# Joint attention pieces, 64x32 tiles for the last block size, and a fixed TensorE order in an RWKV6-then-mixer kernel

## The chip, the cores and the metric

The kernel runs on one core of one Trainium2 chip. The metric is device time in microseconds (us), the median of several runs. The engines are called PE (TensorE), DVE (VectorE), ACT (ScalarE), POOL (GpSimd) and SP (SyncE). PEld is PE's weight load, which overlaps PE's matmuls: in the kernel before PE is busy for 605.2 and PEld for 508.2 us of a span of 635.6.

## The reference, cut to what matters

```python
# batch 4, heads 8, seq 768, head_dim 48; d_model 384, d_tok 256, d_ch 1536, all float32
state = np.zeros((B, H, D, D))
for t in range(S):
    cur = np.einsum('bhd,bhe->bhde', u[None] * kt, vt)
    y[:, :, t] = np.einsum('bhd,bhde->bhe', rt, state + cur)
    state = wt[:, :, :, None] * state + np.einsum('bhd,bhe->bhde', kt, vt)
# then, per batch, with x = y as (B, S, H*D):
h = np.maximum(x.T @ w_tok1, 0) @ w_tok2
u = x + h.T
out = u + np.maximum(u @ w_ch1, 0) @ w_ch2
```

## The kernel before

The attention is cut into 12 units of 256 tokens, three to a batch. A unit has two sets of pieces. `levels` builds its 64x64 blocks of attention weights: a first block, then block sizes 2, 4, 8, 16 and 32, each with 32 small matmuls on tiles of 64x64 of PE ("gram"), a `join` on DVE that multiplies decays into r and k in place, and a `pick` that copies the block out of PSUM, where the kernel's matmuls write. `post` then turns k (`tokens`), makes the state's increments (`carry`), updates the state on DVE (`update`), and makes the output in two matmul pieces (`before`, `within`).

```python
def fours(f):
    for q, j in ((0, 0), (1, 1), (1, 0), (0, 1)):
        f(q, j, slice(q * P, q * P + D), slice(j * T, (j + 1) * T))

def gram(l):
    b = 1 << l
    right = r_.rearrange("p (n two b) -> p n two b", two=2, b=b)[:, :, 1, :]
    g = L["g"] = ps_g.tile([128, 2, 512], f32, name="gram")
    for ca in range(UC * A):
        fours(lambda q, j, rows, cols: pe.matmul(
            g[cols, q, ts(ca, 32)], k_[rows, ds(ca * 128 + j * T, T)],
            right[rows, ts(2 * ca + j, 32 // b), :], start=True, stop=True))

def block(l):
    gram(l)
    join(l, products[l], products[l + 1])
    pick(l)
...
    return [(1.0, tokens), (1.1, carry), (0.1, update), (1.1, before), (1.1, within), ...]   # post
```

A mixing is token mixing with its way back (`back`, tile `h_ps`) and the transposes behind it (`turn`, tile `xT_ps`), then channel mixing in three segments, each with its two matmuls called ups and downs. From the result on, "start-up" is the time to the first downs of the first mixing, and stages 1, 2 and 3 run from there to the heads (starts) of the second, third and last mixing; the last mixing has no attention beside it.

The mixer's part that matters below is the token mixing's way back (`back`, tile `h_ps`) and the transposes behind it (`turn`, tile `xT_ps`). Both take their PSUM from the pool `ps_m`, which has two slots.

```python
def back(c):
    ps = ps_m.tile([128, DM], f32, name="h_ps", tag="m")
    for i in range(DTOK // 128):
        pe.matmul(ps, wtok2[:, i, ts(c, 128)], h1[:, i, :], start=(i == 0), stop=(i == DTOK // 128 - 1))
    x = xs[bt]
    dve.tensor_add(x[:, c, :], x[:, c, :], ps)

def turn(c):
    ps = ps_m.tile([128, DM // 128, 128], f32, name="xT_ps", tag="m")
    for m in range(DM // 128):
        pe.transpose(ps[:, m, :], xs[bt][:, c, ts(m, 128)], ident)
    act.copy(xT[:, :, ts(c, 128)], ps)
...
# one after another: back 0, back 1, turn 0, back 2, turn 1, ... back 5, turn 4, turn 5
```

While one batch is mixed, the next batch's attention is woven into it by estimated cost, and a scheduler then places the instructions of each engine:

```python
att = levels(n)
for i in range(n, n + UB - 1):
    att += woven(levels(i + 1), post(i))
att += post(n + UB - 1)
emit(woven(att, pieces))
```

Of the kernel before, what the change touches and what calls it, by code (L numbers as in the profile page):

```python
# [10 lines left out]
f32 = mybir.dt.float32  # L11
# [7 lines left out]
B, H, S, D = 4, 8, 768, 48  # L19
DM = H * D  # L20
T = 64
C = S // 128
UC = 2
UB = C // UC
NU = B * UB
A = H // 2
P = 64
ROWS = P + D
LEVELS = 6
# [8 lines left out]
def woven(*lists):  # L38

    keyed = []  # L40
    for n, pieces in enumerate(lists):
        total, at = sum(c for c, _ in pieces), 0.0
        for i, (c, f) in enumerate(pieces):
            keyed.append(((at + c / 2) / total, n, i, c, f))
            at += c
    return [(c, f) for *_, c, f in sorted(keyed, key=lambda e: e[:3])]


def emit(pieces):
    for _, f in pieces:  # L50
        f()
# [3 lines left out]
def rwkv6_then_mixer(  # L55
# [21 lines left out]

    nc = tc.nc
    pe, dve, act, pool, sp = nc.tensor, nc.vector, nc.scalar, nc.gpsimd, nc.sync

    const = ctx.enter_context(tc.tile_pool(name="const", bufs=1))
    wts = ctx.enter_context(tc.tile_pool(name="wts", bufs=1))
# [5 lines left out]
    ps_g = ctx.enter_context(tc.tile_pool(name="ps_g", bufs=2, space=bass.MemoryType.PSUM))  # L88
# [32 lines left out]
    for l in range(4):  # L121
        b = 1 << l
# [6 lines left out]
        n, x = (T, 1) if l == 0 else (32, UC * A)  # L129
# [67 lines left out]
    def levels(i):  # L197
        L = live[i] = {}
        r_, k_, w_ = rs[i % 3], ks[i % 3], ws[i % 3]
        at = weights_at[i % 3]  # L200
        at_c = at.rearrange("p q (c a) t -> p q c a t", c=UC)

        products = []

        def begin():
            decay = apool.tile([128, COLS // 2], f32, name="decay")
            L["w"] = apool.tile([128, UC, A, 2], f32, name="w_chunk", bufs=4)
            pool.memset(L["w"], 0.0)
            products.extend([w_, decay, w_[:, :COLS // 4], decay[:, :COLS // 8], w_[:, :COLS // 16],
                             decay[:, :COLS // 32], L["w"].rearrange("p c a j -> p (c a j)")])  # L210

            rp = L["rp"] = apool.tile([128, COLS], f32, name="rp")
            kp = L["kp"] = apool.tile([128, COLS], f32, name="kp", bufs=1)
            both = [(t.rearrange("p (n two) -> p n two", two=2)[:ROWS], x.rearrange("p (n two) -> p n two", two=2)[:ROWS], o)
                    for t, x, o in ((rp, r_, 1), (kp, k_, 0))]
            for t, x, o in both:
                act.copy(t[:, :, o], x[:, :, o])
            for t, x, o in both:
                t, x = (e[:, :, 1 - o].rearrange("p (c a n) -> p c a n", c=UC, a=A) for e in (t, x))
                for a in range(A):  # L220
                    act.mul(t[:, :, a, :], x[:, :, a, :], u_col[:ROWS, a:a + 1])  # L221
# [6 lines that stand above are left out]
        def gram0(c):  # L228
            g = L["g", c] = ps_g.tile([128, 2, 512], f32, name="gram")
            for a in range(A):  # L230
                def one(q, j, rows, cols):
                    tokens = ds((c * A + a) * 128 + j * T, T)
                    pe.matmul(g[cols, q, ts(a, T)], L["kp"][rows, tokens], L["rp"][rows, tokens],  # L233
                              start=True, stop=True)
                fours(one)

        def pick0(c):
            g = L.pop(("g", c))[:, :, :A * T].rearrange("p q (a t) -> p q a t", a=A)
            dve.copy_predicated(out=at_c[:, :, c, :, :], data=g,  # L239
                                mask=masks[0].unsqueeze(1).to_broadcast([128, 2, A, T]))  # L240

        def gram(l):
            b = 1 << l
            right = r_.rearrange("p (n two b) -> p n two b", two=2, b=b)[:, :, 1, :]
            g = L["g"] = ps_g.tile([128, 2, 512], f32, name="gram")
            for ca in range(UC * A):
# [3 lines that stand above are left out]

        def pick(l):
            b = 1 << l
            g = L.pop("g")[:, :, :UC * A * 32]
            if l < 4:
                dst = at.rearrange("p q x (m two b) -> p q (x m) two b", two=2, b=b)[:, :, :, 1, :]
                dve.copy_predicated(  # L256
                    out=dst, data=g.rearrange("p q (m b) -> p q m b", b=b),
                    mask=masks[l].rearrange("p x t -> p (x t)").rearrange("p (m b) -> p m b", b=b)
                    .unsqueeze(1).to_broadcast([128, 2, UC * A * 32 // b, b]))
                return  # L260
            g = g.rearrange("p q (x t) -> p q x t", t=32)
            for p in range(0, 128, 2 * b):
                n = p % T // (2 * b)
                act.copy(at[p:p + b, :, :, n * 2 * b + b:(n + 1) * 2 * b], g[p:p + b, :, :, ts(n, b)])  # L264

        def join(l, w, new):
            b = 1 << l
            n = COLS // (2 * b)
            right = r_.rearrange("p (n two b) -> p n two b", two=2, b=b)[:ROWS, :, 1, :]
            left = k_.rearrange("p (n two b) -> p n two b", two=2, b=b)[:ROWS, :, 0, :]  # L270
            wv = w.rearrange("p (n two) -> p n two", two=2)[:ROWS]
            dve.tensor_mul(left, left, wv[:, :, 1].unsqueeze(2).to_broadcast([ROWS, n, b]))  # L272
            dve.tensor_mul(right, right, wv[:, :, 0].unsqueeze(2).to_broadcast([ROWS, n, b]))
            dve.tensor_mul(new[:ROWS], wv[:, :, 0], wv[:, :, 1])

        def first_block():
            join(0, products[0], products[1])
            for c in range(UC):
                gram0(c)
                pick0(c)  # L280
# [6 lines that stand above are left out]
        pieces = [(0.1, begin), (1.6, first_block)]  # L287
        for l in range(1, LEVELS):
            pieces.append((1.2, lambda l=l: block(l)))
        return pieces  # L290
# [97 lines left out]
    def weight_sums():  # L388
        t1, t2, t4 = w_sums
        dve.tensor_sub(t1, w12, w11)  # L390
        dve.tensor_sub(t2, w22, t1)
        dve.tensor_sub(t4, w21, t2)
# [4 lines left out]
    def mixing(bt):  # L397
# [113 lines left out]
        downs = [first if (bt, s) == (0, 0) else quarters(s) for s in range(S // SEG)]  # L511
        return hiddens, turned, ups, downs


    hiddens, turned, ups, downs = mixing(0)
    hiddens = [list(e) for e in zip(*hiddens)]
# [15 lines left out]
    for bt in range(B):  # L532
        if bt == 0:
            emit(woven(turned, to_ch[:2]))
            both = [f for e in zip(ups[0], ups[1]) for f in e]
            emit(woven(both, to_ch[2:7]))
            emit(woven(downs[0][:-4], to_ch[7:]))
            weight_sums()
            pieces = downs[0][-4:] + [(0.01, weight_difference)] + downs[1] + ups[2] + downs[2]
        else:  # L540
            hiddens, pieces, ups, downs = mixing(bt)
            pieces = [(3.9, lambda h=h: emit(h)) for h in hiddens] + pieces
            for s in range(S // SEG):
                pieces += ups[s] + downs[s]
        n = (bt + 1) * UB
        if n < NU:
            att = levels(n)
            for i in range(n, n + UB - 1):
                att += woven(levels(i + 1), post(i))
            att += post(n + UB - 1)  # L550
            emit(woven(att, pieces))
        else:
            emit(pieces)

# [28 lines left out]
```

## Time and profile before

| | before |
|---|---|
| median, range | 638.11 us, 637.76 to 639.53 (3 runs; 638.46 with a fourth, used from the result on) |
| span of the profiled run | 635.6 us |
| PE busy | 605.2 us, 95% of the span |
| DVE, ACT busy | 341.8 and 198.3 us |
| runs on tiles after the first downs of the first mixing | 92 |

A "run on tiles" is an unbroken row of PE's matmuls on tiles smaller than the array, with full-array matmuls in front and behind. One fp32 matmul is two records in the trace: the 32 of a gram stand there as x64. The page and the timeline are read in the prediction below; the thing to keep is that from 152 us on PE is never idle for long, and that what it loses lies between its instructions, not in its waits.

### The profile page before, as it was taken

What the parts mean: (1) busy time and instruction counts of PE and PEld (TensorE: products, weight loads), DVE (VectorE), ACT (ScalarE), POOL (GpSimd) and SP (SyncE); (2) the same over time, 40 slices, a digit from 0 to 9 for tenths busy, and PEclk for the clock granted to TensorE, in tenths of its full rate; (3) what the DMA queues carried; (4) which work ended last, traced back from release to release, by engine and by line L of the source; (5) the groups of instructions that cost most, each with busy time, mean ns of one, the idle gap of its engine ahead of it and who ended that gap; (6) DMA issues with size and microseconds to landing.
All of it is one profiled execution on the core that took longest, in us unless ns stands there. A gap on an engine that the chain in (4) does not pass through costs nothing.

```text
span 635.6 us, 19813 instructions
## 1 busy us (share of the span) xinstructions
PE 605.2 (95%) x8980; PEld 508.2 (80%) x8980; DVE 341.8 (54%) x743; ACT 198.3 (31%) x476; POOL 7.2 (1%) x32
## 2 busy tenths in 40 slices
PE   3899888999999999999999999999999999999997
PEld 2787566877888876789898886789898895798987
DVE  5889789995656736274184436356155341030404
ACT  7054554520344422421512503430501511212020
POOL 3000000000000000000000000000000000000000
PEclk9999669999999999999999999999999999999999
DMA  8226664700131230101201220000000000000000
GB/s 346 95 78 211 167 184 141 226 31 26 53 103 27 78 102 2 51 2 54 75 3 52 76 76 2 2 2 16 14 2 27 2 14 12 2 1 25 13 13 25
DMA packets 19381, 38.63 MB, mean 61 GB/s; under 512 B 2113, under 2 KB 12865, under 8 KB 19297
## 3 DMA queue, kind: packets, MB, share of 16 engines
q1 hardware_dynamic: 19152, 37.36, 18.3%
q8 instruction: 70, 1.15, 0.8%
q14 instruction: 15, 0.11, 0.1%
q10 hardware_dynamic: 144, 0.00, 0.0%
HBM read 32.64 MB, written 4.72 MB: 59 GB/s over the span
## 4 chain that ended last, share of the span: by engine, by line
PE 90%; ACT 3%; DVE 3%; DMA 2%; issue 1%; SPq 0%; ACTq 0%; DVEq 0%
PE z_ps L427 31%; PE q_ps L461 24%; PE gram L247 10%; PE h_ps L405 6%; PE h_ps L412 5%; PE h_ps L437 2%; PE kv_ps L317 2%; PE gram L233 2%; PE y_ps L367 2%; PE y_ps L354 2%; PE kT_ps L307 1%; ACT at L264 1%; DMA scratch<-in_w_ch_dram 1%; PE xT_ps L419 1%; DMA w<-in_rkw_dram 1%
## 5 line engine op out<-in xcount | busy, mean ns | idle before, releaser
L427 PE MATMUL z_ps<-xT,wch 128*128 128x256 f32 x864 | 198.5, 384 | 0.5 <-ACT xT L420 0.5
L427 PEld LDWEIGHTS z_ps<-xT,wch 128*128 128x128 f32 x864 | 160.4, 190 | 23.3 <-ACT z L429 1.0
L429 ACT ACTIVATE z<-z_ps 128x256 f32<-128x256 f32 x144 | 55.1, 383 | 184.4 <-PE z_ps L427 183.8
L461 PE MATMUL q_ps<-wch,z 128*128 128x192 f32 x528 | 94.9, 330 | 0.0
L247 PEld LDWEIGHTS gram<-r,k 48*64 48x64 f32 x3840 | 74.6, 155 | 23.1 <-issue 15.8
L461 PEld LDWEIGHTS q_ps<-wch,z 128*128 128x128 f32 x528 | 86.1, 190 | 1.4
L247 PE MATMUL gram<-r,k 48*64 48x32 f32 x3840 | 81.6, 237 | 4.6 <-DVE at L256 1.7
L461 PE MATMUL q_ps<-scratch,z 128*128 128x192 f32 x396 | 71.2, 330 | 0.2 <-ACT kT L308 0.2
L461 PEld LDWEIGHTS q_ps<-scratch,z 128*128 128x128 f32 x396 | 64.2, 190 | 1.3 <-ACT kT L308 0.6
L272 DVE TENSOR_TENSOR k<-k,decay 112x512 f32<-112x512 f32 x36 | 24.9, 690 | 62.2 <-PE gram L247 62.2
L453 DVE TENSOR_TENSOR z<-z 128x768 f32<-128x768 f32 x11 | 10.5, 959 | 66.6 <-ACT z L429 66.6
L264 ACT COPY at<-gram 16x256 f32<-16x256 f32 (+1 forms) x72 | 31.2, 434 | 35.3 <-PE gram L247 33.8
L272 DVE TENSOR_TENSOR k<-k,w 112x512 f32<-112x512 f32 x36 | 24.7, 686 | 30.1 <-PE gram L247 24.6
L405 PE MATMUL h_ps<-x,wtok 128*128 128x384 f32 x96 | 39.1, 557 | 1.7 <-ACT x L373 1.6
L412 PE MATMUL h_ps<-h,wtok 128*128 128x384 f32 x96 | 36.2, 505 | 3.4 <-ACT xT L420 1.7
L239 DVE COPY_PREDICATED at<-mask,gram 128x512 f32<-128x512 uint8 x24 | 16.5, 723 | 30.9 <-PE gram L233 30.9
L334 DVE SCALAR_TENSOR_TENSOR state<-state,w_chunk,kv_ps 128x48 f32<-128x48 f32 x160 | 30.5, 256 | 4.4 <-PE kv_ps L317 4.3
L256 DVE COPY_PREDICATED at<-mask,gram 128x512 f32<-128x512 uint8 x36 | 32.3, 897 | 0.0
L233 PE MATMUL gram<-rp,kp 48*64 48x64 f32 x768 | 21.2, 249 | 10.5 <-ACT kp L221 8.0
L233 PEld LDWEIGHTS gram<-rp,kp 48*64 48x64 f32 x768 | 17.4, 154 | 16.9 <-ACT kp L221 10.4
L405 PEld LDWEIGHTS h_ps<-x,wtok 128*128 128x128 f32 x96 | 19.4, 212 | 13.5 <-issue 2.4
L412 PEld LDWEIGHTS h_ps<-h,wtok 128*128 128x128 f32 x96 | 16.9, 192 | 14.3 <-DVE x L414 2.9
(77 smaller groups left out, 522.4 us busy)
## 6 DMA issues: line engine op xcount, KB each, us to landing
scratch<-in_w_ch_dram SPq DMA_DIRECT2D x10, 512.0 KB, 4.5
vt<-in_v_dram SPq DMA_DIRECT2D x12, 384.0 KB, 3.9
out_dram<-o SPq DMA_DIRECT2D x24, 192.0 KB, 1.9
x<-in_w_ch_dram SPq DMA_DIRECT2D x8, 512.0 KB, 4.1
w<-in_rkw_dram SPq DMA_DIRECT2D x18, 192.0 KB, 3.3
k<-in_rkw_dram SPq DMA_DIRECT2D x18, 192.0 KB, 3.1
r<-in_rkw_dram SPq DMA_DIRECT2D x18, 192.0 KB, 3.5
scratch<-in_w_tok_dram SPq DMA_DIRECT2D x4, 512.0 KB, 9.2
```

What stands on the lines that cost most here:

```text
L233: pe.matmul(g[cols, q, ts(a, T)], L["kp"][rows, tokens], L["rp"][rows, tokens], start=True, stop=True)
L239: dve.copy_predicated(out=at_c[:, :, c, :, :], data=g, mask=masks[0].unsqueeze(1).to_broadcast([128, 2, A, T]))
L247: fours(lambda q, j, rows, cols: pe.matmul(g[cols, q, ts(ca, 32)], k_[rows, ds(ca * 128 + j * T, T)], right[rows, ts(2 * ca + j, 32 // b), ...
L256: dve.copy_predicated(out=dst, data=g.rearrange("p q (m b) -> p q m b", b=b), mask=masks[l].rearrange("p x t -> p (x t)").rearrange("p (m ...
L264: act.copy(at[p:p + b, :, :, n * 2 * b + b:(n + 1) * 2 * b], g[p:p + b, :, :, ts(n, b)])
L272: dve.tensor_mul(left, left, wv[:, :, 1].unsqueeze(2).to_broadcast([ROWS, n, b]))
L334: dve.scalar_tensor_tensor(new[:, a], state[bt, g][:, a], L["w"][:, c, a, j:j + 1], got[:, a], op0=ALU.mult, op1=ALU.add)
L405: pe.matmul(sums[i], wtok1[:, c, ts(i, 128)], xs[bt][:, c, :], start=(c == 0), stop=(c == C - 1))
L412: pe.matmul(ps, wtok2[:, i, ts(c, 128)], h1[:, i, :], start=(i == 0), stop=(i == DTOK // 128 - 1))
L427: pe.matmul(ps, wch1[:, m, ts(jt, 128)], xT[:, m, ts(s, SEG)], start=(m == 0), stop=(m == DM // 128 - 1))
L429: act.activation(zs[s][:, jt, :], ps, AF.Relu)
L461: pe.matmul(ps, a[:, j, :], b[:, j, :], start=(j == 0), stop=(j == HJ - 1))
```

## The change

It has three parts. The last block size, 32, is computed in tiles of 64x32, eight at a time instead of four. `beside` makes one piece each of carry and the next unit's first block, of before and its level 1, and of within and its level 2, so that PE goes into tiles once for two pieces; a stage's first unit then has its levels done a stage earlier. And `in_order` chains PE's instructions in emission order from the second mixing on, so that the scheduler can't take the joint pieces apart.

```diff
--- before.py
+++ after.py
@@ -77,6 +77,20 @@
 
     nc = tc.nc
     pe, dve, act, pool, sp = nc.tensor, nc.vector, nc.scalar, nc.gpsimd, nc.sync
+
+    block = nc.cur_bb.bb
+    behind = mybir.DependencyInfo(mybir.DependencyClass.NoSync, mybir.DependencyReason.DATA)
+
+    def in_order(pieces):
+
+        last = next(ins.name for ins in reversed(block.instructions) if ins.engine == pe.engine)
+        for _, f in pieces:
+            done = len(block.instructions)
+            f()
+            for ins in block.instructions[done:]:
+                if ins.engine == pe.engine:
+                    tc.add_manual_dep(ins, last, behind, reason="TensorE's order")
+                    last = ins.name
 
     const = ctx.enter_context(tc.tile_pool(name="const", bufs=1))
     wts = ctx.enter_context(tc.tile_pool(name="wts", bufs=1))
@@ -241,6 +255,15 @@
 
         def gram(l):
             b = 1 << l
+            if l == LEVELS - 1:
+
+                g = L["g"] = ps_g.tile([128, 2, 512], f32, name="gram")
+                for a in range(A):
+                    for c, j, q in ((0, 0, 0), (0, 1, 1), (1, 0, 0), (1, 1, 1), (0, 0, 1), (0, 1, 0), (1, 0, 1), (1, 1, 0)):
+                        at_t, rows = (c * A + a) * 128 + j * T, slice(q * P, q * P + D)
+                        pe.matmul(g[ds(j * T + c * b, b), q, ts(a, b)], k_[rows, ds(at_t, b)], r_[rows, ds(at_t + b, b)],
+                                  start=True, stop=True)
+                return
             right = r_.rearrange("p (n two b) -> p n two b", two=2, b=b)[:, :, 1, :]
             g = L["g"] = ps_g.tile([128, 2, 512], f32, name="gram")
             for ca in range(UC * A):
@@ -250,7 +273,14 @@
 
         def pick(l):
             b = 1 << l
-            g = L.pop("g")[:, :, :UC * A * 32]
+            g = L.pop("g")
+            if l == LEVELS - 1:
+                g = g[:, :, :A * b].rearrange("p q (a t) -> p q a t", t=b)
+                for c in range(UC):
+                    for p in range(0, 128, T):
+                        act.copy(at[p:p + b, :, ts(c, A), b:], g[ds(p + c * b, b)])
+                return
+            g = g[:, :, :UC * A * 32]
             if l < 4:
                 dst = at.rearrange("p q x (m two b) -> p q (x m) two b", two=2, b=b)[:, :, :, 1, :]
                 dve.copy_predicated(
@@ -511,6 +541,16 @@
         downs = [first if (bt, s) == (0, 0) else quarters(s) for s in range(S // SEG)]
         return hiddens, turned, ups, downs
 
+    def beside(after, ahead):
+
+        tokens, carry, update, before, within, *loads = after
+        begin, first, *rest = ahead
+
+        def one(*pieces):
+            return (sum(c for c, _ in pieces), lambda: emit(pieces))
+
+        return [begin, tokens, one(carry, first), update, one(before, rest[0]), one(within, rest[1]), *loads, *rest[2:]]
+
 
     hiddens, turned, ups, downs = mixing(0)
     hiddens = [list(e) for e in zip(*hiddens)]
@@ -544,11 +584,10 @@
                 pieces += ups[s] + downs[s]
         n = (bt + 1) * UB
         if n < NU:
-            att = levels(n)
-            for i in range(n, n + UB - 1):
-                att += woven(levels(i + 1), post(i))
-            att += post(n + UB - 1)
-            emit(woven(att, pieces))
+            att = levels(n) if bt == 0 else []
+            for i in range(n, n + UB):
+                att += beside(post(i), levels(i + 1)) if i + 1 < NU else post(i)
+            (emit if bt == 0 else in_order)(woven(att, pieces))
         else:
             emit(pieces)
 
```

## The prediction

> **What bounds the kernel now.** I read the busy table first, then the chain of work that ended last, then busy time by stage, then the waits, and last TensorE's (PE's) own sequence.
>
> ```profile
> PE 605.2 (95%) x8980; PEld 508.2 (80%) x8980; DVE 341.8 (54%) x743; ACT 198.3 (31%) x476; POOL 7.2 (1%) x32
> ```
>
> ```profile
> PE 90%; ACT 3%; DVE 3%; DMA 2%; issue 1%; SPq 0%; ACTq 0%; DVEq 0%
> ```
>
> ```profile
> 152.00:233.00 81.00, 80.34 (x1868) 69.71 (x1867) 51.33 (x124) 27.98 (x70) 0.34 (x3) 1.00 0.24 70
> 233.00:379.00 146.00, 144.96 (x2231) 122.03 (x2231) 70.08 (x155) 45.80 (x114) 0.23 (x2) 1.00 0.15 44
> 379.00:525.00 146.00, 144.90 (x2250) 122.24 (x2249) 66.61 (x149) 40.06 (x98) 0.00 (x0) 1.00 0.03 10
> 525.00:636.00 111.00, 105.59 (x532) 92.03 (x530) 24.54 (x45) 18.64 (x47) 0.00 (x0) 0.99 0.04 13
> ```
>
> The third fence has, by stretch: length, then busy time of PE, weight loads, VectorE (DVE), ScalarE (ACT), GpSimd. The stretches are the first mixing's rest with attention units 3 to 5 (I call it stage 1), the second and third mixing with units 6 to 8 and 9 to 11 (stages 2 and 3), and the last mixing alone. From 152 us on PE has work at all times, so a microsecond saved on PE there is a microsecond of the program, if no new wait comes. The waits of PE after 150 us:
>
> ```profile
> PE h_ps L412 <- DVE x L414: 1.3, 4, 0.4
> PE gram L247 <- DVE r L273: 1.2, 2, 0.6
> PE z_ps L427 <- ACT xT L420: 0.5, 2, 0.3
> PE kT_ps L307 <- DVE k L272: 0.4, 1, 0.4
> ```
>
> They are about 4 us in all, and the 1.3 lies in the last mixing, which doesn't change. So the time isn't in waits. It is in how PE's work is arranged:
>
> ```profile
> 321.44 2.11 PE L461 MATMUL q_ps<-scratch,z 128*128 128x192 f32 x12
> 323.48 1.13 PE L247 MATMUL gram<-r,k 48*64 48x32 f32 x64
> 324.55 2.22 PE L461 MATMUL q_ps<-wch,z 128*128 128x192 f32 x12
> 326.60 2.11 PE L461 MATMUL q_ps<-scratch,z 128*128 128x192 f32 x12
> ...
> 512.39 1.14 PE L317 MATMUL kv_ps<-vt,kT 64*64 64x48 f32 x48
> 513.46 3.84 PE L461 MATMUL q_ps<-scratch,z 128*128 128x192 f32 x22
> ...
> 560.06 2.11 PE L461 MATMUL q_ps<-wch,z 128*128 128x192 f32 x12
> 562.01 2.11 PE L461 MATMUL q_ps<-scratch,z 128*128 128x192 f32 x12
> ```
>
> Columns: start in us, length, engine, line, tile, shape, count; one fp32 matmul of the program is two records here. Read starts, not lengths. Twelve full-array matmuls take 562.01-560.06 = 1.95 us when others follow, but 2.04 us in front of a run on tiles (323.48-321.44) and 2.05 us behind one (326.60-324.55). The run itself lasts 1.07 us. So a lone run of 64 costs 1.07+0.09+0.10 = 1.26 us. In the single records, 15 steps of 58.4 ns separate the 16 groups of four (four tiles, 6.7 ns apart inside a group). That leaves 1.26-16x0.0584 = 0.33 us that is paid for going into tiles and back. Of the 92 runs on tiles after 150 us 80 show it to 0.01 us, 8 some 0.05 less, and 4 have a wait in them.
>
> ```profile
> 173.33 1.15 PE L317 MATMUL kv_ps<-vt,kT 64*64 64x48 f32 x64
> 174.30 1.10 PE L247 MATMUL gram<-r,k 48*64 48x32 f32 x64
> 175.33 2.22 PE L461 MATMUL q_ps<-wch,z 128*128 128x192 f32 x12
> ```
>
> Here two runs stand side by side: 175.33-173.33 = 2.00 us for both. The switch is paid once; two lone runs would be 2x1.26 = 2.52 against 2.00+0.19 = 2.19 us. The saving is 0.33 us for each run joined to another.
>
> [...] a tile takes its next matmul after 58.4 ns for moving widths 32, 48 and 64 alike, and the 48 above, on two tiles at first, need the same 1.07 us as 64. [...]
>
> **The change, part by part.**
>
> *Joint pieces and PE in emission order.* I counted runs on tiles between full-array work in the built programs. Stage 1: 27 before, 29 after; stage 2: 33 and 18; stage 3: 32 and 15. In all 92 and 62. (Stage 1 isn't put in order, and takes level 0 to 5 of unit 6 from stage 2, so it grows.) 30 x 0.334 us = **-10.0 us**. All lie on PE's path. Before, the scheduler also cut blocks of 32 into 3+29, 13+19 or 6+26; cut blocks lose their grouping in fours: bodies of 0.120+0.924 us against 0.916 for a whole one, or 0.429+0.559. Summed over the cut blocks, 1.4 us before; three such cuts (0.4) remain in stage 1: **-1.0 us**.
>
> *Last block size in tiles of 64x32.* The count of matmuls stays 32 per unit (64 records), but weights have 32 columns and there are eight tiles. Estimate: a full load starts 108 ns before the next, one of 64 columns 58.4, so 32 columns should take about 34 ns. Eight issues at 6.7 ns are 54 ns, which is longer, so issue sets the pace: 8 groups x 54 = 0.43 us against 16 x 58.4 = 0.93. That is 0.49 us less in each of nine blocks from stage 1 on, 4.4 us. No run on eight tiles is in this trace, so I count **-4.0 us**. Evacuation on ACT goes from 2 copies of 0.575 us to 4 of some 0.36 (from the 16x256 form): +0.3 us per unit, off PE's path, with ACT at a third.
>
> *Start-up (0 to 92 us).* Order is unchanged; units 0 to 2 get the small tiles too. A group of four takes 107 ns at the low clock there, so the two blocks near 34 us would save some 2.5 us of PE. But the transposes at 37.13 us then wait for ACT's copies, which free PSUM and now end hardly sooner (0.3 us). The block of unit 2 at 69.9 us may give another half: **-0.8 us**.
>
> *New waits.* The fixed order takes away the scheduler's filling. (a) At the head of stages 2 and 3 the mixing goes h, turn, h, turn; each h waits 0.32 us for the addition before it, as in the last mixing. Before, pieces of gram were put there, and yet 1.0 us per stage was lost (PE waiting for r and xT at 256.7 and 403.1 us). Walking the new order against DVE's with measured lengths, I get 1.5 us in stage 2, where join and mask copy of level 1 delay an addition by about 0.4, and 1.3 in stage 3: +0.8 net. (b) Where stage 2 begins, kT's transposes stand directly behind the last gram and need its join: +0.8 us, against 0.4 for a similar wait before. (c) Stage 1 holds four units' levels instead of three: DVE goes from 51 to about 65 us of 83. My walk through its first two units shows 0.4 us of waits. For what I can't see I add 0.3 us. Sum: **+1.9 us**. The other new spacings are wide: between kv with gram 0 and the next joint piece stand 4 to 10 us of mixing, against 3 us for the state update (16 of 0.17 to 0.19 us start to start) and 1.3 for two masks.
>
> Sum: -10.0-1.0-4.0-0.8+1.9 = -13.9; 638.1-13.9 = **624.2 us**.
>
> **Rivals.** *Waits eat it*: the joint piece makes DVE do state, masks and join in one burst, and PE can't go elsewhere. For it speaks the burst, about 6 us of DVE per unit; against it the stage sums (DVE under half in stages 2 and 3) and the spacings. It would add 4 to 7 us: 628 to 631. *Small tiles don't pay*: eight tiles don't load side by side, or instructions can't be fed at 6.7 ns. For it speaks that groups never hold more than four here; against it, that the two-tile part shows tiles setting the pace. Then 4 us are missing: 628. *DVE bounds stage 1*, with 65 of 83 us and chains level by level: 3 us more, 627. *The switch isn't saved*[...]: against it the 2.00 us above, a seam of 64- and 48-row work. It would be 634.
>
> **Range and chances.** The first two terms are counted and measured, and sure to about 1 us. Small tiles may give 0 to 4.4, waits 1 to 7, start-up -1.5 to +1.5 (its clock changes between half and full). Misses lie more on the slow side: 620.5 to 630.5 us. The 2% line is 625.3, one microsecond above my number, so faster 0.59, same 0.39, slower 0.02.
>
> **What would show it.** In the profile after: PE's busy time about 590 us; lone small-tile runs lasting about 0.57 us from start to next start instead of 1.07; joined runs of 128 at 2.0 us; stages 2 and 3 together about 18 us shorter and stage 1 about 5 longer, since it takes over unit 6's levels (some 5.6 us of blocks); waits of PE on x and k of 3 to 4 us after 150 us. I'm wrong if PE waits more than 7 us there, if the small-tile runs still last 1 us, or if joined runs still show 0.33 us at their seam.

## The result, and the profile after

| | before | after |
|---|---|---|
| median | 638.46 us (4 runs, 637.76 to 639.53) | 627.67 us (4 runs, 626.83 to 629.03) |
| ratio | | 0.983, interval 0.981 to 0.986 |
| span of the profiled run | 635.6 | 625.1 |
| start of the first ups, the first downs | 105.4, 136.9 | 103.0, 134.4 |
| start of stage 2, of stage 3, of the last mixing | 231.7, 377.9, 523.9 | 236.1, 377.1, 513.4 |

The change saves 10.8 us, 1.7%, so it falls within 2%. A ratio here is the mean time of one kernel's runs over that of the other's of the same rounds, so it is not quite the ratio of the medians quoted. In every run the time is some 1.7 us above the span.

The page's first and fourth part after (busy time; shares of the chain of work that ended last):

```profile
PE 590.0 (94%) x8980; PEld 499.3 (80%) x8980; DVE 341.7 (55%) x743; ACT 202.5 (32%) x500; POOL 7.2 (1%) x32
...
PE 87%; DVE 7%; ACT 3%; issue 1%; DMA 1%; SPq 0%; ACTq 0%; DVEq 0%
```

The same number of matmuls (8980 records) keeps PE busy for 15 us less. The chain has moved from PE (90 to 87%) towards DVE (3 to 7%): the first sign that DVE now holds PE up more often. Busy time by stretch, columns as in the prediction:

```profile
152.00:235.00 83.00, 81.52 (x2140) 71.52 (x2133) 60.80 (x143) 35.60 (x93) 0.34 (x3) 1.00 0.26 74
235.00:377.00 142.00, 139.86 (x2254) 119.84 (x2253) 70.28 (x156) 46.89 (x121) 0.22 (x2) 1.00 0.15 41
377.00:513.00 136.00, 133.80 (x1870) 114.51 (x1869) 54.38 (x127) 34.49 (x86) 0.00 (x0) 1.00 0.03 11
513.00:626.00 113.00, 107.05 (x538) 93.10 (x536) 24.91 (x46) 18.64 (x47) 0.00 (x0) 0.99 0.04 13
```

Stages 2 and 3 now have about 2.2 us each in which PE is not busy (142.00-139.86 and 136.00-133.80), against 1.04 and 1.10 before. PE's waits after 150 us (engine, tile and line that waited, what it waited for: us in total, times, longest):

```profile
PE h_ps L442 <- DVE x L444: 4.0, 10, 0.9
PE kT_ps L337 <- DVE k L302: 1.3, 2, 0.8
PE xT_ps L449 <- DVE x L444: 0.6, 2, 0.3
PE h_ps L442 <- ACT xT L450: 0.6, 1, 0.6
```

The wait of h for an addition on DVE was four times 0.3 to 0.4 us before, all in the last mixing; now there are ten. A joint run and a lone run of the small tiles on PE:

```profile
263.64 1.15 PE L397 MATMUL y_ps<-vt,at 64*64 64x48 f32 x64
264.61 1.10 PE L270 MATMUL gram<-r,k 48*64 48x32 f32 x64
265.64 0.70 PE L457 MATMUL z_ps<-xT,wch 128*128 128x256 f32 x2
...
280.01 0.76 PE L264 MATMUL gram<-r,k 48*32 48x32 f32 x64
280.70 0.48 PE L457 MATMUL z_ps<-xT,wch 128*128 128x256 f32 x1
```

The joint run lasts 265.64-263.64 = 2.00 us from start to next start, as predicted. The small-tile run lasts 280.70-280.01 = 0.69 us instead of the 1.07 of before; going in and out of it costs about 0.32 us, against 0.33 for tiles of 64x64.

To see where the time went, I sorted every step from one PE start to the next by what stands on its two sides. A full-array step counts at its own undisturbed length (215.8 ns for 256 moving columns, 162.5 for 192, 322.5 for 384; 150 for a transpose, which is some 40 ns too long: undisturbed ones in these traces start 109 ns apart), steps inside a run on tiles count as such, what a step is longer in front of a run, behind it, or as the run's last is "in and out", and what is left over is waits. Since a transpose is set too long, the waits' row lies too low in every column alike, below zero where little waits; read its differences. Stages 2 and 3 together, in us; before has there the levels of a unit that the others do in stage 1, and its waits for r in front of a gram fall under "in and out":

| stages 2 and 3 | before | after | the same without fixed order (e_no_order) |
|---|---|---|---|
| inside runs on tiles | 50.4 | 42.7 | 43.4 |
| in and out of tiles | 23.6 | 11.1 | 15.9 |
| full array at its own pace | 218.7 | 217.5 | 217.5 |
| waits and rest | -0.5 | 5.9 | -1.2 |
| sum | 292.2 | 277.2 | 275.6 |

Going in and out of tiles fell by about what was counted: over stages 1 to 3 it went from 33.2 to 22.1 us (the last part below takes before's waits for r out of this). What came in its place is 6.4 us of waits. The last column, a kernel told below, has almost all of the gain without them.

### The profile page after: what moved, and what is told of

It reads as the page before. It is cut to its first block, busy times and chain, and to the rows that moved or that the text cites. A ratio compares the mean times of both kernels' runs of the same rounds, so it can differ in the third digit from the quotient of the medians. Undisturbed runs are those within 1.5% of the kernel's fastest.

```text
span 625.1 us, 19850 instructions
## 1 busy us (share of the span) xinstructions
PE 590.0 (94%) x8980; PEld 499.3 (80%) x8980; DVE 341.7 (55%) x743; ACT 202.5 (32%) x500; POOL 7.2 (1%) x32
## 4 chain that ended last, share of the span: by engine, by line
PE 87%; DVE 7%; ACT 3%; issue 1%; DMA 1%; SPq 0%; ACTq 0%; DVEq 0%
PE z_ps L457 30%; PE q_ps L491 25%; PE gram L270 8%; PE h_ps L435 5%; PE h_ps L442 5%; PE h_ps L467 3%; PE kv_ps L347 2%; PE y_ps L397 2%; PE y_ps L384 2%; PE gram L247 1%; DVE x L444 1%; PE gram L264 1%; ACT at L281 1%; DVE at L253 1%; PE kT_ps L337 1%
## 5 line engine op out<-in xcount | busy, mean ns | idle before, releaser
L457 PE MATMUL z_ps<-xT,wch 128*128 128x256 f32 x864 | 195.3, 382 | 0.1
L491 PE MATMUL q_ps<-wch,z 128*128 128x192 f32 x528 | 93.6, 329 | 0.1
L270 PEld LDWEIGHTS gram<-r,k 48*64 48x64 f32 x3072 | 59.6, 155 | 11.4 <-issue 5.9
L270 PE MATMUL gram<-r,k 48*64 48x32 f32 x3072 | 64.3, 236 | 3.2 <-DVE at L286 1.7
L483 DVE TENSOR_TENSOR z<-z 128x768 f32<-128x768 f32 x11 | 10.5, 959 | 63.5 <-ACT z L459 63.5
L364 DVE SCALAR_TENSOR_TENSOR state<-state,w_chunk,kv_ps 128x48 f32<-128x48 f32 x160 | 30.8, 256 | 15.9 <-PE kv_ps L347 15.8
L435 PE MATMUL h_ps<-x,wtok 128*128 128x384 f32 x96 | 37.5, 541 | 2.0 <-ACT x L403 1.6
L444 DVE TENSOR_TENSOR x<-x,h_ps 128x384 f32<-128x384 f32 x24 | 13.3, 555 | 37.4 <-PE h_ps L442 37.2
L286 DVE COPY_PREDICATED at<-mask,gram 128x512 f32<-128x512 uint8 x36 | 32.3, 898 | 0.0
L247 PE MATMUL gram<-rp,kp 48*64 48x64 f32 x768 | 19.7, 247 | 10.8 <-ACT kp L235 8.1
L294 ACT COPY at<-gram 16x256 f32<-16x256 f32 x48 | 17.5, 364 | 35.1 <-PE gram L270 33.8
```

What stands on the lines that cost most here:

```text
L247: pe.matmul(g[cols, q, ts(a, T)], L["kp"][rows, tokens], L["rp"][rows, tokens], start=True, stop=True)
L270: fours(lambda q, j, rows, cols: pe.matmul(g[cols, q, ts(ca, 32)], k_[rows, ds(ca * 128 + j * T, T)], right[rows, ts(2 * ca + j, 32 // b), ...
L286: dve.copy_predicated(out=dst, data=g.rearrange("p q (m b) -> p q m b", b=b), mask=masks[l].rearrange("p x t -> p (x t)").rearrange("p (m ...
L364: dve.scalar_tensor_tensor(new[:, a], state[bt, g][:, a], L["w"][:, c, a, j:j + 1], got[:, a], op0=ALU.mult, op1=ALU.add)
L435: pe.matmul(sums[i], wtok1[:, c, ts(i, 128)], xs[bt][:, c, :], start=(c == 0), stop=(c == C - 1))
L457: pe.matmul(ps, wch1[:, m, ts(jt, 128)], xT[:, m, ts(s, SEG)], start=(m == 0), stop=(m == DM // 128 - 1))
```

## The experiments

"Before" is always the kernel before, run on the same chip in the same rounds: 637.98 us for a, d, e, f; 638.33 for c, h, i, j; 638.42 for b, g, n. The counts of runs on tiles are for the time after the first downs of the first mixing.

### a_tiles_only: the small tiles alone

```diff
 # the kernel before
 def gram(l):
+    if l == LEVELS - 1:
+        g = L["g"] = ps_g.tile([128, 2, 512], f32, name="gram")
+        for a in range(A):
+            for c, j, q in (...):            # the eight tiles of 64x32, as in the change
+                ...
+        return
 def pick(l):
+    if l == LEVELS - 1: ...                  # four copies on ACT, as in the change
```

> The kernel before with the 64x32 tiles for block size 32 as the only edit; weave and TensorE's order as before. Runs on tiles stay at 92 after the first mixing. My theory, from the two traces: the tiles give 0.38 us in each of nine later blocks (3.4 us) and 2.4 us in the start-up, so 638.4 - 5.8 = 632.6 us (ratio 0.991). Rival 1, the start-up gain comes from something else, such as a clock that recovered sooner by chance: 635.0. Rival 2, the gain is mine to misread and the tiles pay nothing on TensorE's path, the gain lies in the joining: 638. Rival 3, the prediction's own terms, 4.0 + 0.8: 633.6, too near to the theory to be told apart by the time alone, so I read the blocks: the theory wants lone blocks of 64 records that last about 0.56 us plus 0.1 each side, the prediction 0.43.

Measured: 633.63 us (633.36 to 634.89), ratio 0.993 (0.991 to 0.995), 4.4 us less than before. The first ups start at 104.8 us and the first downs at 136.3, each 0.6 us earlier than before. Lone blocks lie at 0.69 us from start to next start, as in the changed kernel, not at the prediction's 0.57. So the tiles pay, nearer to the prediction's 4.8 us in all than to my 5.8. In this profile stages 1 to 3 are only 2.0 us shorter than before's (385.0 against 387.0): steps inside the runs fell by 3.3 us, but PE's list has new waits (q_ps for ACT's kT 1.0 us, kT_ps for ACT's z 0.6). What I had put down to the start-up (2.4 us in one pair of profiles) isn't theirs alone: kernels whose start-up is built alike (before, b, c and d) begin the first downs at 136.9, 136.8, 137.9 and 135.8 us in their profiles, so one profile can't tell a start-up to better than 1 us.

### b_joint_only: the joint pieces alone

```diff
 # the kernel before
-            att = levels(n)
-            for i in range(n, n + UB - 1):
-                att += woven(levels(i + 1), post(i))
-            att += post(n + UB - 1)
+            att = levels(n) if bt == 0 else []
+            for i in range(n, n + UB):
+                att += beside(post(i), levels(i + 1)) if i + 1 < NU else post(i)
```

> The kernel before with the joint pieces alone: no small tiles, the scheduler places TensorE's instructions. Built order: 78 runs on tiles after the first mixing instead of 92, 34 cut blocks instead of 27. Theory: 14 x 0.334 = 4.7 us come off, and the waits for r and x at the heads of stages 2 and 3 go with the levels that stood there (about 1 us per stage), cuts give 0.5 back: 638.2 - 6.2 = 632.0 us; e_no_order less the tiles' 4.4 says the same, 631. Rival 1, the joint pieces pay only with the small tiles: 636. Rival 2, VectorE's burst behind a joint piece makes TensorE wait here too: 635 to 638.

Measured: 631.07 us (629.77 to 633.20), ratio 0.988 (0.986 to 0.991), 7.4 us less. The joint pieces are the largest part of the change and need neither the tiles nor the order. 14 runs less are 4.7 us. Before had waits for r in front of gram at the heads of stages 2 and 3 (1.2 us of idle in its list of waits), and they are not in this kernel's list. With a's 4.4 the sum is 11.8, and e, which has both parts, saves 11.4: the two add up.

### c_order_only: the fixed order alone

```diff
 # the kernel before
-            emit(woven(att, pieces))
+            (emit if bt == 0 else in_order)(woven(att, pieces))
```

> The kernel before with the emission order of TensorE fixed from the second mixing on, as the only edit: old weave, no small tiles. Built order: 80 runs on tiles after the first mixing instead of 92, 14 cut blocks instead of 27. Theory: 12 x 0.334 = 4.0 us and 13 x 0.07 = 0.9 us come off, but the heads of stages 2, 3 and of each h, turn pair wait as in the changed kernel, 5.5 to 7 us by the accounting of e_no_order against the changed kernel. So 638.0 - 4.9 + 6.2 = 639.3 us: same or a little slower. Rival 1, the prediction's view, that order costs some 1.9 us: 635. Rival 2, the waits come with the joint pieces' burst on VectorE, not with the order: 633 to 634.

Measured: 641.70 us (640.30 to 642.54), ratio 1.005 (1.003 to 1.006): 3.4 us slower than before. The runs fell from 92 to 80 as built. PE's longest waits from 150 us on:

```profile
PE h_ps L426 <- DVE x L428: 2.9, 8, 0.4
PE z_ps L441 <- ACT xT L434: 2.6, 2, 1.3
PE y_ps L368 <- DVE state L348: 2.5, 2, 1.3
```

These three alone are 8.0 us of idle, where before's list had 1.3 for h on x, 0.5 for z on xT and none for y on state. No joint piece is in this kernel, so the waits come with the order itself. The theory's 639.3 was 2.4 us too low, since it didn't know of the waits of y and z; both rivals fall.

### d_no_tiles: the change without the small tiles

```diff
 # the changed kernel, without the two branches for l == LEVELS - 1 in gram and pick
-            if l == LEVELS - 1: ...
```

> The changed kernel without the 64x32 tiles: joint pieces and emission order stay. Theory: the tiles' part comes back whole, 627.7 + 5.8 = 633.5 us, and start-up (first ups, first downs) falls back to 105.4 and 136.9 us. Joining and order alone are then worth 638.4 - 633.5 = 4.9 us: 30 runs x 0.334 = 10.0 and 0.7 for cuts, less some 5.5 to 6 us of new waits. Rival 1, the tiles' copies on ScalarE cause part of the new waits: then taking them away costs less than in the other direction, 631 us. Rival 2, the tiles were what made the joined blocks short, and the order alone is worth nothing: 638.

Measured: 632.83 us (631.03 to 633.32), ratio 0.991 (0.989 to 0.993). Joining with order saves 5.2 us against 7.4 for joining without it (b): here the order costs about 2 us by the medians and 1.4 by stages 1 to 3 of the profiles (382.2 against 380.8); the intervals of the two ratios just overlap. The tiles are worth 632.83-627.67 = 5.2 us in this surrounding. The start-up fell back by 1.4 us and not by the 2.5 expected (first downs at 135.8 us), so a pair of profiles doesn't settle its share; the last part below averages over more of them.

### e_no_order: the change without the fixed order

```diff
 # the changed kernel
-            (emit if bt == 0 else in_order)(woven(att, pieces))
+            emit(woven(att, pieces))
```

> The changed kernel with its joint pieces and tiles, but TensorE's instructions placed by the scheduler everywhere. Built order: 78 runs on tiles after the first mixing instead of 62, 34 cut blocks instead of 17. Theory: 16 runs x 0.334 = 5.3 us and 17 cuts x 0.07 = 1.2 us more, and the waits that the fixed order brought (about 4 us of the 5.5) fall away: 627.7 + 6.5 - 4 = 630.2 us. Rival 1, the new waits come from VectorE's burst behind the joint pieces and stay with any order: 627.7 + 6.5 = 634.2. Rival 2, the fixed order costs more than it saves: under 627.

Measured: 626.63 us (624.47 to 627.68), ratio 0.981 (0.979 to 0.983). It is 1.0 us under the changed kernel's 627.67. The two intervals overlap and the runs were made at different times, so a real cost of the order isn't shown by this pair of times alone; that the order brings no clear saving is. The profiles' stages 2 and 3 differ by 1.6 us (277.2 against 275.6). Rival 2 comes nearest. The table above shows why: without the order there are 48 runs on tiles in stages 2 and 3 instead of 33, and going in and out costs 4.8 us more, with 0.7 more inside the runs, but 7.1 us of waits are gone. PE at the head of stage 3, without the order:

```profile
393.20 0.49 PE L435 MATMUL xT_ps<-ident,x 128*128 128x128 f32 x3
393.62 0.78 PE L370 MATMUL y_ps<-state,r 48*64 48x48 f32 x22
394.33 1.56 PE L428 MATMUL h_ps<-h,wtok 128*128 128x384 f32 x4
395.72 0.49 PE L435 MATMUL xT_ps<-ident,x 128*128 128x128 f32 x3
396.14 0.45 PE L370 MATMUL y_ps<-state,r 48*64 48x48 f32 x16
396.53 0.91 PE L428 MATMUL h_ps<-h,wtok 128*128 128x384 f32 x2
```

The scheduler cut the joint piece (y, then gram) into parts, y's in 22, 16 and 9 records, and put one between each turn and the next h. (The last line of such a view is cut off at the window's end: its count and length aren't whole.) From h to h that takes 396.53-394.33 = 2.20 us with 16 records of y in it. The changed kernel at the same place, with DVE's instructions:

```profile
391.61 0.60 DVE L364 SCALAR_TENSOR_TENSOR state<-state,w_chunk,kv_ps 128x48 f32<-128x48 f32 x3
...
392.13 0.54 DVE L444 TENSOR_TENSOR x<-x,h_ps 128x384 f32<-128x384 f32 x1
...
392.73 1.56 PE L442 MATMUL h_ps<-h,wtok 128*128 128x384 f32 x4 [0.93 <-DVE x L444]
...
394.93 0.59 PE L442 MATMUL h_ps<-h,wtok 128*128 128x384 f32 x1 [0.32 <-DVE x L444]
```

Here h to h takes 394.93-392.73 = 2.20 us as well, with nothing in it but the transposes. The cuts that I had counted as a loss were the scheduler's use of a wait that is there anyway. The first of these waits is longer (0.93 us), because the addition stands on DVE behind the state update that belongs to the joint piece.

### f_turn_in_gram_banks: a second slot for h

```diff
 # the changed kernel
-            ps = ps_m.tile([128, DM // 128, 128], f32, name="xT_ps", tag="m")
+            ps = ps_g.tile([128, 2, 512], f32, name="gram")[:, 0, :DM].rearrange("p (m t) -> p m t", t=128)
```

> The changed kernel with one edit: the mixing's transposed tile takes its PSUM from the pool of the grams instead of the pool that h uses, so that two h can stand ahead of VectorE's additions. Theory: the ten waits of h for an addition in stage 2, stage 3 and the last mixing (4.0 us together) and some of the start-up's shrink to nearly nothing: 627.7 - 4 = 623.7 us, 622 to 625. Rival 1, the wait only moves on: the transposes behind need the same addition's result, so TensorE waits there instead and the time is the same, 627 to 628. Rival 2, the grams now wait for a slot that the turn holds: 629 or more.

Measured: 620.43 us (618.63 to 621.26), ratio 0.971 (0.969 to 0.973), 7.2 us under the changed kernel. That is more than all the idle in its ten waits, 4.0 us. The reason shows where nothing else runs, in the last mixing. PE in the changed kernel, where h takes turns with the transposes for two slots:

```profile
524.71 1.56 PE L442 MATMUL h_ps<-h,wtok 128*128 128x384 f32 x4 [0.32 <-DVE x L444]
526.11 0.49 PE L449 MATMUL xT_ps<-ident,x 128*128 128x128 f32 x3
526.92 0.59 PE L442 MATMUL h_ps<-h,wtok 128*128 128x384 f32 x1 [0.32 <-DVE x L444]
```

And with the transposes in a gram's banks:

```profile
521.45 1.46 PE L442 MATMUL h_ps<-h,wtok 128*128 128x384 f32 x4
522.74 0.49 PE L449 MATMUL gram<-ident,x 128*128 128x128 f32 x3
523.07 1.46 PE L442 MATMUL h_ps<-h,wtok 128*128 128x384 f32 x4
```

From h to h the step is 526.92-524.71 = 2.21 us with the wait and 523.07-521.45 = 1.62 without: the wait costs 0.59 us, though its idle column says 0.32. Ten waits with 0.27 us more than their idle are 4.0+2.7 = 6.7 of the 7.2 us. Of the missing 0.27, 0.16 lie in the transposes: three take 0.49 us to their end by the trace, but the next matmul that needn't wait starts 523.07-522.74 = 0.33 us after the first of them. The other 0.11 lie in the matmuls behind the wait (526.11-524.71 = 1.40 us against 522.74-521.45 = 1.29). So an idle counted from the end that the trace gives is too short here: 0.32 us of idle for a loss of 0.59.

The last mixing as a whole went from 108.0 to 105.2 us. Stages 2 and 3 went from 277.2 to 272.3, all of it in the waits' row (5.9 to 1.0). Of start-up and stage 1 together one profile says 2.2 us more. Part of it is the scheduler's: with the new pool it left 128 tile records (two blocks) for stage 1 that the changed kernel has before the first downs, so stage 1 is 3.3 us longer (105.0 against 101.7) and the start-up only 1.1 shorter. The profiled run (span 619.5) also had a clock of 0.85 in the first 105 us against 0.92 in the changed kernel's, so I take nothing from the start-up. h, i, j and n share these two blocks in stage 1. Both rivals fall.

### h_turn_free_order: the second slot, without the fixed order

```diff
 # f_turn_in_gram_banks
-            (emit if bt == 0 else in_order)(woven(att, pieces))
+            emit(woven(att, pieces))
```

> f_turn_in_gram_banks without the fixed order. With the turn in the grams' banks h no longer waits for an addition, whoever orders TensorE, so what is left of the fixed order is its saving: 63 runs on tiles with it, 71 without, 16 cuts against 25. Theory: 8 x 0.334 = 2.7 and 9 x 0.07 = 0.6 us more, less some 0.6 us of waits: 620.4 + 2.7 = 623.1 us, that is 3.5 us under e_no_order. Rival 1, the fixed order still has costs that I don't see: 619 to 620.5. Rival 2, the scheduler's filling hid the wait of h anyway, so the bank is worth nothing without the order: 626.6, as e_no_order.

Measured: 620.55 us (617.74 to 621.38), ratio 0.971 (0.969 to 0.973): the same as f within the spread. So the theory's 623.1 was wrong and rival 1 right. By the accounting of stages 2 and 3, leaving the order costs 2.0 us of going in and out (13.1 against 11.1) and 0.3 inside the runs, and brings 2.4 us of waits (-1.4 against 1.0). Even with h free of its wait, other waits remain that only a free order fills: 1.6 us of idle of kT for k in f's list, 1.1 in this one's. The bank is worth about as much without the order as with it (626.63-620.55 = 6.1 us against 7.2), so rival 2 falls: what the scheduler filled, it filled at the price of a switch.

### i_hidden_ahead: something in front of the transposes of k

```diff
 # f_turn_in_gram_banks
+            if bt:
+                in_order(pieces[:1])
+                pieces = pieces[1:]
             (emit if bt == 0 else in_order)(woven(att, pieces))
```

> f_turn_in_gram_banks with the first chunk of the token mixing put ahead of the attention's pieces at the start of stages 2, 3 and of no others, so that the transposes of k no longer stand directly behind the last join. Theory: the waits of kT for k there (0.8 us in stage 2, less in stage 3) and of h1 for kT's copy (0.3) go: about 1.2 us, 619.2 us. Rival, the head only moves the wait to where the hidden chunks need x, or to a later join: 620.4 unchanged, or up to 1 us slower.

Measured: 620.57 us (619.91 to 621.82), ratio 0.972 (0.970 to 0.974). No gain; the rival holds. The wait of kT for k went from 1.6 us of idle to 0.8, but waits of gram for r (0.2 to 0.6) and of the transposes for ACT's copy (0 to 0.6) came in its place.

### j_order_from_first: the fixed order in stage 1 too

```diff
 # f_turn_in_gram_banks
-            (emit if bt == 0 else in_order)(woven(att, pieces))
+            in_order(woven(att, pieces))
```

> f_turn_in_gram_banks with the fixed order in stage 1 too. Built order: 23 runs on tiles there instead of 30, 10 cut blocks in all instead of 16. Theory: 7 x 0.334 = 2.3 and 6 x 0.07 = 0.4 us come off; stage 1 carries four units' levels and VectorE is busy for 73 of its 98 us, so I expect 1 to 2 us of new waits on r and k: 620.4 - 2.7 + 1.5 = 619.2 us. Rival 1, stage 1 is bound by VectorE's chains and the fixed order there costs 4 us or more: 622 to 625. Rival 2, no wait comes: 617.7.

Measured: 624.63 us (621.09 to 627.74), ratio 0.978 (0.975 to 0.981): 4.2 us slower than f, with a wider spread. Stage 1 (the first downs to the head of stage 2) takes 111.3 us instead of 105.0. The list has new waits of y for state (2.5 us of idle) and of gram for r (2.7). Rival 1 holds in its time. Seven runs less were bought with 6.3 us more of stage. Not all of that is waiting: in this profile alone the granted TensorE clock was 0.5 from 160.1 to 163.5 us and from 173.7 to 177.2, soon after waits of 1.51 and 1.39 us, while the other twelve traces show full clock from 93 us until PE's work is done. Twelve matmuls of q_ps take 162.31-159.17 = 3.14 and 177.50-173.82 = 3.68 us there instead of 1.95, so by my estimate some 2.9 of the 6.3 us are clock. Whether the lower clock has to do with the waits, or the wider spread with either, isn't shown.

### n_first_level_joined_free: one more level joined

```diff
 # h_turn_free_order
-        return [begin, tokens, one(carry, first), update, one(before, rest[0]), one(within, rest[1]), *loads, *rest[2:]]
+        return [begin, tokens, one(first, carry, rest[0]), update, one(before, rest[1]), one(within, rest[2]), *loads, *rest[3:]]
```

> h_turn_free_order with the second level joined to the first piece as well: carry between first block and level 1, before with level 2, within with level 3. Built order: 59 runs on tiles after the first mixing instead of 71, 21 cuts instead of 25. By switches alone 12 x 0.334 = 4.0 us come off: 616.5. My theory says less: level 1 needs two masks and a join of VectorE (some 3 us) behind the first block, and carry covers 1.1 us of them; where the scheduler has full-array work at hand it will fill, which brings the run back. So 618 to 621 us. Rival: the built order is not what the chip can keep, TensorE waits about 1.5 us in each of nine units: 630 or more.

Measured: 627.12 us (625.10 to 627.87), ratio 0.981 (0.979 to 0.984): 6.6 us slower than h, outside what I expected. The trace has the 59 runs that were built, so the scheduler did not bring runs back; it left PE waiting. Steps inside runs grew by 3.5 us over stages 1 to 3, and there are new waits, most of them without a releaser that the profile shows (3.9 us of idle). What these stand for I can't say. That level 1 stands too close behind the first block's masks and join fits the growth inside the runs; I didn't test it further.

### g_tiles_in_halves: why a small-tile block is not shorter

```diff
 # the changed kernel
-            for a in range(A):
+            for a in range(A // 2 * half, A // 2 * (half + 1)):   # gram(5) now in two pieces, half 0 and half 1
...
+            if l == LEVELS - 1:
+                pieces.append((0.6, lambda l=l: gram(l, 0)))
```

> The changed kernel with its block of 64x32 tiles cut into two halves of 32 records, with full-array work of the mixing between them. In the changed kernel such a block of 64 records starts its first 32 some 6 ns apart and the rest 16.7 ns apart. Theory, supply: [...] both halves, each of 32, run through in about 0.2 us from first to last start. Rival, the tiles: the second half of the heads lies in columns of PSUM or on rows that hold it up; then the second half still takes 0.5 us. Time by the theory: 7 runs more, 2.3 us, less 9 x 0.16 = 1.4 us, and 6 more cuts 0.4: 629 us.

Measured: one run, 632.82 us (span 631.1, state unknown). As a time it is inconclusive, since its start-up alone lies 3.5 us behind the changed kernel's (first downs at 138.0 us). PE around two halves:

```profile
284.91 0.36 PE L266 MATMUL gram<-r,k 48*32 48x32 f32 x32
285.19 1.56 PE L461 MATMUL z_ps<-xT,wch 128*128 128x256 f32 x6
286.69 0.35 PE L266 MATMUL gram<-r,k 48*32 48x32 f32 x32
286.97 0.43 PE L495 MATMUL q_ps<-wch,z 128*128 128x192 f32 x1
```

Each half takes 0.28 us from start to next start, 0.56 for both, against 0.69 for the whole block. In the single records of all twelve lone halves the first and the last start lie 0.162 to 0.167 us apart, in the second half as in the first, so the rival falls. In the whole block of the changed kernel the first 32 records span 163 ns, 5.3 from start to start on average, then come two steps of 77 and 32 ns, and the last 30 steps take 291 ns, 9.7 ns on average. (What I expected says 16.7 ns for these: I had read the longer of their steps, which mostly take turns with steps of 0.) So 32 records go at the first pace, and 32 more do so too when 1.5 us of full-array work stand between (286.69-285.19), but not directly behind the first. What holds these back, the supply of my theory or something else, isn't shown.

### The versions side by side

| kernel | median, us | against before |
|---|---|---|
| c: fixed order alone | 641.70 | +3.4 |
| a: small tiles alone | 633.63 | -4.4 |
| d: joint pieces and order | 632.83 | -5.2 |
| b: joint pieces alone | 631.07 | -7.4 |
| the change: all three | 627.67 | -10.8 |
| n: h with one more level joined | 627.12 | -11.3 |
| e: joint pieces and tiles | 626.63 | -11.4 |
| j: f with order in stage 1 | 624.63 | -13.7 |
| i: f with a chunk ahead | 620.57 | -17.8 |
| h: joint pieces, tiles, second slot | 620.55 | -17.8 |
| f: the change and second slot | 620.43 | -17.6 |

f, h and i can't be told apart; they beat both kernels, by 2.8 to 2.9% against before. h is the simplest: it has no fixed order.

## Why the prediction was right or wrong, point by point

The time, 627.67, lies inside the range and 3.5 us above the number; the saving was 10.8 us instead of 13.9, and the result fell on the other side of the 2% line from where the larger chance was put. One pair of profiles (spans 635.6 and 625.1) splits the saving like this, in us:

| | predicted | measured |
|---|---|---|
| going in and out of tiles, start-up left out | -10.0 | -9.2 |
| inside the runs (cuts 1.0, small tiles 4.0) | -5.0 | -3.5 |
| start-up | -0.8 | -2.4 |
| waits, net | +1.9 | +4.6 |
| sum | -13.9 | -10.5 |

Before had two gram runs at the heads with waits for r in front of them and for xT behind; each cost 1.32 us of in and out instead of 0.35. These 1.9 us are counted here under waits, as the prediction did. The start-up missed the other way from the rest: 1.6 us of the nearness of the sum is luck.

**Joint pieces and order, 10.0 us.** The mechanism and its count are right: 62 runs were measured, 2.00 us for a joint run, and 11.1 us less in going in and out over stages 1 to 3 (1.9 of it before's waits for r, so 9.2 for the runs). What was wrong is to take two causes as one sum. Of the 30 runs saved, 14 come from the joint pieces and 16 from the order. The first 14 were worth more than their 4.7 us, 7.4 us (b), since before's waits for r went with them. The other 16 were worth 5.3 us on paper and nothing in the end (e), since they were bought with waits.

**Cuts, 1.0 us.** Steps inside the runs did get shorter with the order (43.4 to 42.7 us in stages 2 and 3, 72.1 to 70.7 in stages 1 to 3), but the premise that a cut is only a loss was wrong. At the heads a cut is what fills a wait.

**Small tiles, 4.0 us, and start-up, 0.8.** Together 4.8; alone they gave 4.4 us (a), taken out of the change 5.2 (d). Right in size as a sum, but the split was off. Over stages 1 to 3 the profiles with tiles are only 2.0 us (a against before), 3.2 (the change against d) and 3.4 (e against b) shorter, while the medians of these pairs differ by 4.4, 5.2 and 4.4. What is left, 1.0 to 2.4 us, is my estimate for the start-up; the first downs come at 136.8 us on average in the four profiles without tiles (before, b, c, d) and at 135.0 in three with them (a, e, the change). That the clock is low near 34 us, as the prediction says, is read from PE's steps: groups of four start 107 ns apart there, as they do at a granted clock of 0.5 from 64.8 to 75.1 us, against 58.4 at full clock; the profile itself reads 1.00 for the first 38 us. The mechanism was only half right: the first 32 records of a block start 5.3 ns apart on average, under the 6.7 assumed, but the second half comes after a gap of 109 ns (77+32) and at 9.7 ns; that issue sets the pace, as the estimate had it, isn't shown. A block saves 1.07-0.69 = 0.38 us, not 0.49, so nine blocks give 3.4.

**New waits, 1.9 us.** This is the step that failed, +4.6 us net instead of +1.9: "each h waits 0.32 us for the addition before it". I took the idle column of a PE wait for its cost. From start to start it is 0.59 us. Waits and rest in stages 2 and 3 grew from -0.5 to 5.9 us; before's waits for r, which the row doesn't hold, are taken off in the table above. Stage 1 is not the cause: its waits' row stays at -0.4 us (-0.5 before). The sum of printed idle after 150 us went only from 3.9 us (the six rows before) to 6.8 (five rows, the fifth of 0.3), so it passed the test that I had set (wrong if PE waits more than 7 us), and that test was too lenient for the same reason. That k's transposes stand behind the last join was foreseen (0.8 us, in the trace 0.8).

**Rivals.** The nearest was "waits eat it", 628 to 631, with the burst on DVE as its cause. The waits are there, but the burst explains only the longer ones such as the 0.93 us above. The others are the two PSUM slots that h shares with the transposes, as f shows, and the order, which forbids filling. "Small tiles don't pay" was part right in that the second half of a block starts 9.7 ns apart and not 6.7. DVE did not bound stage 1 in the changed kernel; only with the order there too (j) did its waits come. The result of every experiment was correct. Stage 1 grew by 101.7-94.9 = 6.8 us instead of 5, and stages 2 and 3 shrank by 14.9 us instead of 18.

## What to carry to other kernels

Price a wait of TensorE from start to start, against the same pair of instructions where nothing waits, and not by the idle that a profile prints. Before fixing an engine's order to save switches, look at what the scheduler puts between the pieces that it cuts: a switch of 0.33 us that fills a wait of 0.59, the costs measured here, is a gain. Take the wait away first, here with another PSUM slot; then the order from the second mixing on hardly matters (f and h).
